# Two-head softmax denominators: one broadcast per head, and new hop lengths for the order planner

## The chip, the cores and the metric

The kernel runs on one core of a Trainium2 chip. The metric is the device time of one execution in microseconds (us), and lower is better. The engines of the core are PE (TensorE, matmuls), DVE (VectorE), ACT (ScalarE), POOL (GpSimd) and SP (SyncE), which issues every DMA of this kernel from one queue. Each engine takes its instructions in the order in which they stand in its own program, and an instruction that waits holds up all behind it on that engine.

## What is computed

Causal attention over 2 batches of 12 heads (448 tokens, head size 64), followed by two feed-forward networks on 896 tokens of width 768, all in float32:

```
scores = q @ k.T / 8, masked above the diagonal, minus the row maximum
attn   = exp(scores) / (sum(exp(scores)) + 1e-9)
x      = attn @ v                      # heads side by side: 896 x 768
xn     = x / sqrt(mean(x*x) + 1e-6) * rms_g
y      = (silu(xn @ w_gate) * (xn @ w_val)) @ w_out     # inner width 1536
h      = y @ w_in
out    = max(0.01*h, h) @ w_out2                        # inner width 2048
```

The weights arrive as float64 and are turned on the chip into pairs of float32 (a high and a low part); each product of the two networks is three matmuls.

## The kernel before, in words

**Attention.** The 24 heads are worked on as 12 pairs; pairs 0 to 5 are batch 0, pairs 6 to 11 batch 1. One pair i passes through these steps:

1. `load_pair`: SP loads `qk` (448 KB) and `v` (256 KB) into one of five buffers. `round_pair`: ACT casts q and k (L268).
2. `maxima` (L281, L289): PE multiplies q by k into two PSUM banks, DVE takes masked row maxima into `m`. `maxima_rows`: PE transposes them (L315), DVE copies them to `mt` (L318), SP writes them to DRAM (`md`, L320) and reads them back as one row for each head (`mrow`, L324).
3. `exponents`: PE adds the row of maxima (L339) and the product k by q (L343), ACT takes the exponential into `p` (L364), POOL clears what lies beyond the diagonal (L370, L374).
4. `attend`: PE sums `p` over keys by a matmul with ones (L401) and multiplies `p` by v (L386). ACT copies the sums to `sm` (L421). Then comes a trip over DRAM which spreads the 2 x 448 sums over 64 partitions, so that the reciprocal is short, and spreads the results over all partitions: SP stores `sd` (L423) and loads `st` in two transfers (L427); DVE adds and takes the reciprocal into `r` (L431, L434); SP stores `rd` (L436) and loads the broadcast `rb` (L439): 128 partitions, 64 with the 448 values of each head. POOL multiplies the pair's output by `rb` (L446), ACT squares it (L454), and POOL adds the squares to `acc` (L457). The last pair has its reciprocals taken on DVE (L416, L418), without this trip.

Such a trip is four transfers, each of which waits for the one before: sums to `sd`, `sd` to `st`, `r` to `rd`, `rd` to `rb`. Buffers of this trip are rings of four: `rd_134` and `rb_138` belong to pairs 0, 4 and 8, `rd_135` and `rb_139` to 1, 5 and 9, `rd_136` and `rb_140` to 2, 6 and 10, `rd_137` and `rb_141` to 3 and 7.

**Norm.** After the last pair of a batch, `norm` sums `acc` over partitions on PE (L475), goes over DVE, POOL, PE (L482) and ACT to a scale for each token, and DVE, ACT and POOL write `xn` (L502 to L512).

**Networks.** Matmuls at L571, L572 and L573, eighteen for a block of 128 outputs of one batch. The first four weight blocks (`hl_69` to `hl_72`) are loaded and converted during attention. Their 72 matmuls for batch 0 need only the norm of batch 0, so PE has them to do while batch 1 ends. Those for batch 1 begin after the second norm, and the further weights are converted by ACT, DVE and POOL (L187 to L197) from then on.

**What sets the order.** No engine program is written out by hand. Every step is handed to a planner (`Order`) with its engine, a cost, a rank, and `late`, the time from the end of an issue until its result is there. `emit` plays the program with these numbers, always takes the step that can start first (of those ready, the one of lowest rank), and emits the instructions in that order. At run time the engines keep the order, and wait for each other by semaphores only. So a changed cost or `late` moves instructions on all engines.

Of the kernel before, what the change touches and what calls it, by code (L numbers as in the profile page):

```python
# [18 lines left out]
class Order:  # L19
# [12 lines left out]
    def add(self, eng, cost, fn, r=(), w=(), rank=0.0, late=0.0, mode=None, at=0.0):  # L32
        n = len(self.steps)
        deps = set()
        for k in r:
            deps.update(self.written.get(k, ()))
        for k in w:
            deps.update(self.written.get(k, ()))
            deps.update(self.read.get(k, ()))
        for k in w:  # L40
            self.written[k] = [n]
            self.read[k] = []
        for k in r:
            if k not in w:
                self.read.setdefault(k, []).append(n)
        self.steps.append((eng, cost, fn, deps, rank, late, mode, at))
        return n
# [48 lines left out]
def causal_attention_two_ffns(  # L96
# [23 lines left out]
    nc = tc.nc  # L120
    P = 128
    NPAIR, _, _, S = qk.shape
    D = 64
# [14 lines left out]
    add = od.add  # L138
# [15 lines left out]
    late = {}  # L154
# [17 lines left out]
    def weight(key, rank, at=0.0):  # L172
        n = slot[key]
        src = queue[n][1]
        w = src.shape[1]
        raw, x, hl = raws[n % NRAW], xs32[n % NX], hls[n % NHL]
        kr, kx, kh = ("raw", n % NRAW), ("x", n % NX), ("hl", n % NHL)
        words = raw.bitcast(U32).rearrange("p (n t) -> p n t", t=2)
        top, low = words[:, :w, 1], words[:, :w, 0]
        tf = raw.bitcast(F32).rearrange("p (n t) -> p n t", t=2)[:, :w, 1]  # L180
        xb = x.bitcast(U32)[:, :w]
        add("SP", 0.5, lambda: nc.sync.dma_start(out=raw[:, :w], in_=src),
            w=[kr], rank=rank - 30, late=6.0, at=at)

        add("ACT", 0.85, lambda: nc.scalar.activation(x[:, :w], tf, AF.Abs), r=[kr], w=[kx], rank=rank)  # L187
        add("DVE", 0.62, lambda: nc.vector.tensor_scalar(  # L188
            x[:, :w], x[:, :w], LEAST, MOST, ALU.max, ALU.min), r=[kx], w=[kx], rank=rank)
        add("DVE", 0.6, lambda: nc.vector.tensor_scalar(  # L190
            xb, xb, 3, 0x3FFFFFF8, ALU.logical_shift_left, ALU.bitwise_and), r=[kx], w=[kx], rank=rank)
        add("DVE", 1.0, lambda: nc.vector.scalar_tensor_tensor(  # L192
            xb, top, 0xC0000000, xb, ALU.bitwise_and, ALU.bitwise_or), r=[kr, kx], w=[kx], rank=rank)
        add("DVE", 1.0, lambda: nc.vector.scalar_tensor_tensor(  # L194
            xb, low, 29, xb, ALU.logical_shift_right, ALU.bitwise_or), r=[kr, kx], w=[kx], rank=rank)
        add("ACT", 0.85, lambda: nc.scalar.copy(hl[:, 0, :w], x[:, :w]), r=[kx], w=[kh], rank=rank)  # L196
        add("POOL", 1.95, lambda: nc.gpsimd.tensor_tensor(  # L197
            out=hl[:, 1, :w], in0=x[:, :w], in1=f32(hl[:, 0, :w]), op=ALU.subtract),
            r=[kx, kh], w=[kh], rank=rank)
# [13 lines left out]
    NQ, NR, NM, NB = 5, 3, 4, 4  # L213
# [5 lines left out]
    mt = ring(NM, [2 * NC, C], F32R, "mt")  # L219
    md = ring(NM, [2, NC, C], F32, "md", dram)  # L220
# [5 lines left out]
    sms = ring(2, [P, S], F32, "sm")  # L226
# [3 lines left out]
    sd = ring(NB, [2, 2, QA, QB], F32, "sd", dram)  # L230
    sts = ring(NB, [2 * QA, 2, QB], F32, "st")
    rs = ring(NB, [2 * QA, QB], F32, "r")
    rd = ring(NB, [2, QA, QB], F32, "rd", dram)
    rbs = ring(NB, [P, S], F32, "rb")
# [9 lines left out]
    SP, ST, AV, SM = banks[0:2], banks[2:6], banks[6], banks[7]  # L244
# [14 lines left out]

    def load_pair(i, at):  # L260
        add("SP", 0.5, lambda: nc.sync.dma_start(out=qks[i % NQ], in_=qk[i]),
            w=[("qk", i % NQ)], rank=10 * i - 30, late=3.0, at=at)
        add("SP", 0.5, lambda: nc.sync.dma_start(out=vs[i % NQ], in_=v[i]),
            w=[("v", i % NQ)], rank=10 * i - 20, late=3.0, at=at)

    def round_pair(i):
        t, o = qks[i % NQ], qkr[i % NR]
# [44 lines left out]
    def maxima_rows(i):  # L312
        keys = [("m", i % NM, j, c) for j in range(2) for c in range(NC)]
        m = m32[i % NM]
        add("PE", 0.12, lambda: nc.tensor.transpose(  # L315
            out=SM[:2 * NC, :C], in_=m.rearrange("p j c -> p (j c)"), identity=ident[:C, :C]),
            r=keys, w=["sm"], rank=10 * i - 29, mode=128)
        add("DVE", 0.15, lambda: nc.vector.tensor_copy(mt[i % NM], SM[:2 * NC, :C]),  # L318
            r=["sm"], w=[("mt", i % NM)], rank=10 * i - 29)
        add("SP", 0.45, lambda: nc.sync.dma_start(  # L320
            out=md[i % NM].rearrange("j c p -> (j c) p"), in_=f32(mt[i % NM])),
            r=[("mt", i % NM)], w=[("md", i % NM)], rank=10 * i - 160, late=2.1)
        for j in range(2):
            add("SP", 0.4, lambda j=j: nc.sync.dma_start(  # L324
                out=f32(MS[i % NM][j * D:j * D + 1, :]),
                in_=md[i % NM][j].rearrange("c p -> (c p)").unsqueeze(0)),
                r=[("md", i % NM)], w=[("ms", i % NM, j)], rank=10 * i - 160, late=2.1)

    def exponents(i):
        t = qks[i % NQ]  # L330
# [47 lines left out]
    def attend(i):  # L378
        b, hp = divmod(i, NP)
        x = x32[:, hp, b * S:(b + 1) * S]  # L380
# [28 lines left out]
        for kb in range(KB):  # L409
            add("PE", pw[kb] * 0.00165 + 0.04, lambda kb=kb: values(kb),  # L410
                r=[("p", i % 2, 0, kb), ("p", i % 2, 1, kb), ("v", i % NQ)], w=["av"], rank=10 * i + 5,
                mode=128)
        if last:
            for h in range(2):
                n = slice(h * S // 2, (h + 1) * S // 2)
                add("DVE", 0.4, lambda n=n: nc.vector.tensor_scalar(  # L416
                    rbs[i % NB][:, n], SM[:, n], 1e-9, None, ALU.add), r=["sm"], w=[("rb", i % NB, h)], rank=0)
                add("DVE", 1.9, lambda n=n: nc.vector.reciprocal(rbs[i % NB][:, n], rbs[i % NB][:, n]),  # L418
                    w=[("rb", i % NB, h)], rank=0)
        else:  # L420
            add("ACT", 0.57, lambda: nc.scalar.copy(sms[i % 2], SM[:, :S]), r=["sm"], w=[("sms", i % 2)],  # L421
                rank=10 * i + 5)
            add("SP", 0.45, lambda: nc.sync.dma_start(  # L423
                out=sd[i % NB].rearrange("j h a b -> (j h) (a b)"), in_=sms[i % 2][0:P:32, :]),
                r=[("sms", i % 2)], w=[("sd", i % NB)], rank=10 * i - 60, late=2.1)
            for j in range(2):
                add("SP", 0.45, lambda j=j: nc.sync.dma_start(  # L427
                    out=sts[i % NB][j * QA:(j + 1) * QA], in_=sd[i % NB][j].rearrange("h a b -> a h b")),
                    r=[("sd", i % NB)], w=[("sts", i % NB, j)], rank=10 * i - 60, late=2.1)
            st = sts[i % NB]  # L430
            add("DVE", 0.15, lambda: nc.vector.scalar_tensor_tensor(  # L431
                out=rs[i % NB], in0=st[:, 0], scalar=1e-9, in1=st[:, 1], op0=ALU.add, op1=ALU.add),
                r=[("sts", i % NB, 0), ("sts", i % NB, 1)], w=[("r", i % NB)], rank=10 * i - 20)
            add("DVE", 0.25, lambda: nc.vector.reciprocal(rs[i % NB], rs[i % NB]),  # L434
                w=[("r", i % NB)], rank=10 * i - 20)
            add("SP", 0.45, lambda: nc.sync.dma_start(  # L436
                out=rd[i % NB].rearrange("j a b -> (j a) b"), in_=rs[i % NB]),
                r=[("r", i % NB)], w=[("rd", i % NB)], rank=10 * i - 60, late=2.1)
            add("SP", 0.45, lambda: nc.sync.dma_start(  # L439
                out=rbs[i % NB],  # L440
                in_=rd[i % NB].rearrange("j a b -> j (a b)").unsqueeze(1).to_broadcast([2, D, S])),
                r=[("rd", i % NB)], w=[("rb", i % NB)], rank=10 * i - 60, late=2.4)
        if i + 1 < NPAIR:
            add("ACT", 0.57, lambda: nc.scalar.copy(x, AV[:, :S]), r=["av"], w=[("x", b, hp)],
                rank=10 * i + 5)
            add("POOL", 1.1, lambda: nc.gpsimd.tensor_tensor(out=x, in0=x, in1=rbs[i % NB], op=ALU.mult),  # L446
                r=[("rb", i % NB)], w=[("x", b, hp)], rank=10 * i + 26)
        else:
            add("DVE", 0.65, lambda: nc.vector.tensor_tensor(
                out=x, in0=AV[:, :S], in1=rbs[i % NB], op=ALU.mult),  # L450
                r=["av", ("rb", i % NB, 0), ("rb", i % NB, 1)], w=[("x", b, hp)], rank=10 * i + 26)
        a = acc[:, b * S:(b + 1) * S]
        sq = sqs[i % 2] if hp else a
        add("ACT", 0.57, lambda: nc.scalar.activation(sq, x, AF.Square), r=[("x", b, hp)],  # L454
            w=[("sq", i % 2) if hp else ("acc", b)], rank=10 * i + 27)
        if hp:
            add("POOL", 1.1, lambda: nc.gpsimd.tensor_tensor(out=a, in0=a, in1=sq, op=ALU.add),  # L457
                r=[("sq", i % 2)], w=[("acc", b)], rank=10 * i + 27)
# [315 lines left out]
```

## Time and profile before

| what | value |
|---|---|
| median of 3 runs | 679.12 us (675.7 to 685.01) |
| the profiled execution | 676.31 us |
| its span, first to last instruction | 674.6 us |
| time outside the span | 1.7 us |
| PE busy | 630.5 us, 93% of the span |
| DVE, ACT, POOL busy | 395.7, 249.8, 198.8 us |
| mean granted PE clock | 0.947 of full speed |
| DMA | 68.26 MB, mean 101 GB/s |

The profile's time line falls into three stages: attention up to about 167 us, the second norm and the start of the networks up to about 209 us, and from there to the end a stretch of matmuls. A granted clock of 1.00 is 2.4 GHz, 0.50 is 1.2 GHz. A row of the time line gives the start, the duration, engine, line, operation, tiles and count, and in brackets how long the engine stood idle before it and what ended that.

### The profile page before, as it was taken

How to read it: one execution, taken by the hardware profiler on the slowest of the kernel's cores; microseconds unless marked ns; L12 is line 12 of the kernel's file. 1: busy time of each engine (PE TensorE's matmuls, PEld its weight loads, DVE VectorE, ACT ScalarE, POOL GpSimd, SP SyncE). 2: the span in 40 equal slices, each digit the busy share in tenths (PEclk: the TensorE clock that was granted, in tenths of full speed). 3: DMA queues.
4: the chain of work that ended last, by engine and by line, in shares of the span. 5: the costliest groups of instructions: out<-in, count | busy, mean ns of one | idle time of the engine just before them, and what ended most of it. 6: DMA issues, size and time to landing. Idle time of an engine off the chain costs nothing.

```text
span 674.6 us, 8621 instructions
## 1 busy us (share of the span) xinstructions
PE 630.5 (93%) x3280; PEld 542.0 (80%) x3280; DVE 395.7 (59%) x668; ACT 249.8 (37%) x410; POOL 198.8 (29%) x158
## 2 busy tenths in 40 slices
PE   7968968799399999999999999999999999999997
PEld 4544445467388999999999999999999999999997
DVE  6665424513279977655666445579999984443400
ACT  3553423431154343333432332345455452232210
POOL 0154324542323232223232222233233222323210
PEclk9896777789689999999999999999999999999999
DMA  7362221002304432333224232223223324334000
GB/s 249 116 184 67 82 71 32 30 17 62 108 12 175 142 141 101 133 116 119 94 93 141 97 134 97 95 94 137 98 93 123 97 78 138 111 133 153 28 27 29
DMA packets 19848, 68.26 MB, mean 101 GB/s; under 512 B 4762, under 2 KB 7774, under 8 KB 19806
## 3 DMA queue, kind: packets, MB, share of 16 engines
q1 hardware_dynamic: 19806, 67.70, 30.2%
q8 instruction: 26, 0.43, 0.3%
q14 instruction: 16, 0.13, 0.1%
HBM read 64.78 MB, written 2.91 MB: 100 GB/s over the span
## 4 chain that ended last, share of the span: by engine, by line
PE 68%; DVE 2%; issue 0%; ACT 0%; POOL 0%; POOLq 0%; ACTq 0%
PE bank L573 23%; PE bank L571 23%; PE bank L572 23%; DVE x L192 1%; POOL hl L197 0%; DVE x L194 0%; DVE T L630 0%; DVE sg L625 0%; ACT T L628 0%; ACT sg L623 0%; DVE x L190 0%; DVE x L188 0%; ACT sg L724 0%; POOLq L197 0%; ACTq L724 0%
## 5 line engine op out<-in xcount | busy, mean ns | idle before, releaser
L197 POOL TENSOR_TENSOR hl<-x,hl 128x768 fp32r<-128x768 f32 (+1 forms) x70 | 139.4, 1992 | 340.0 <-ACT hl L196 334.6
L571 PE MATMUL bank<-xn,hl 128*128 128x448 f32 x288 | 107.3, 372 | 1.9 <-ACT xn L505 1.9
L572 PE MATMUL bank<-xn,hl 128*128 128x448 f32 x288 | 107.0, 372 | 1.5 <-POOL xn L512 1.1
L573 PE MATMUL bank<-xn,hl 128*128 128x448 f32 x288 | 106.6, 370 | 0.3 <-POOL hl L197 0.3
L187 ACT ACTIVATE x<-raw 128x768 f32<-128x768 f32 (+1 forms) x70 | 61.8, 884 | 104.8 <-POOL hl L197 104.8
L188 DVE TENSOR_SCALAR x<-x 128x768 f32<-128x768 f32 (+1 forms) x70 | 39.4, 562 | 93.8 <-ACT x L187 93.8
L192 DVE SCALAR_TENSOR_TENSOR x<-raw,x 128x768 uint32<-128x768 uint32 (+1 forms) x70 | 87.0, 1243 | 2.2
L196 ACT CAST hl<-x 128x768 fp32r<-128x768 f32 (+1 forms) x70 | 56.8, 812 | 48.5 <-PE bank L572 44.8
L573 PE MATMUL bank<-y,hl 128*128 128x448 f32 x192 | 70.1, 365 | 0.0
L571 PE MATMUL bank<-y,hl 128*128 128x448 f32 x192 | 70.1, 365 | 0.0
L572 PE MATMUL bank<-G,hl 128*128 128x448 f32 x192 | 70.1, 365 | 0.0
L571 PE MATMUL bank<-G,hl 128*128 128x448 f32 x192 | 70.1, 365 | 0.0
L573 PE MATMUL bank<-G,hl 128*128 128x448 f32 x192 | 70.1, 365 | 0.0
L572 PE MATMUL bank<-y,hl 128*128 128x448 f32 x192 | 70.1, 365 | 0.0
L194 DVE SCALAR_TENSOR_TENSOR x<-raw,x 128x768 uint32<-128x768 uint32 (+1 forms) x70 | 65.4, 934 | 1.1
L572 PEld LDWEIGHTS bank<-xn,hl 128*128 128x128 f32 x288 | 55.2, 192 | 6.8 <-POOL xn L512 1.4
L571 PEld LDWEIGHTS bank<-xn,hl 128*128 128x128 f32 x288 | 55.1, 191 | 6.6 <-ACT xn L505 2.1
L573 PEld LDWEIGHTS bank<-xn,hl 128*128 128x128 f32 x288 | 55.1, 191 | 5.0 <-POOL hl L197 0.6
L289 DVE CUSTOM_DVE_ANT_0 bank<-bank,maskw 112x224 f32<-112x224 f32 (+2 forms) x96 | 42.2, 466 | 28.5 <-PE bank L281 27.2
L572 PE MATMUL bank<-T,hl 128*128 128x448 f32 x144 | 52.6, 365 | 0.0
L571 PE MATMUL bank<-T,hl 128*128 128x448 f32 x144 | 52.6, 365 | 0.0
L573 PE MATMUL bank<-T,hl 128*128 128x448 f32 x144 | 52.6, 365 | 0.0
(79 smaller groups left out, 939.3 us busy)
## 6 DMA issues: line engine op xcount, KB each, us to landing
raw<-in_out SPq DMA_DIRECT2D x24, 768.0 KB
raw<-in_in SPq DMA_DIRECT2D x16, 768.0 KB
raw<-in_gate SPq DMA_DIRECT2D x12, 768.0 KB
raw<-in_val SPq DMA_DIRECT2D x12, 768.0 KB
qk<-in_qk SPq DMA_DIRECT2D x12, 448.0 KB
v<-in_v SPq DMA_DIRECT2D x12, 256.0 KB
raw<-in_out SPq DMA_DIRECT2D x6, 512.0 KB
out<-sg SPq DMA_DIRECT2D x12, 224.0 KB
```

Of the source, the lines that this page charges most:

```text
L187: add("ACT", 0.85, lambda: nc.scalar.activation(x[:, :w], tf, AF.Abs), r=[kr], w=[kx], rank=rank)
L188: add("DVE", 0.62, lambda: nc.vector.tensor_scalar(x[:, :w], x[:, :w], LEAST, MOST, ALU.max, ALU.min), r=[kx], w=[kx], rank=rank)
L192: add("DVE", 1.0, lambda: nc.vector.scalar_tensor_tensor(xb, top, 0xC0000000, xb, ALU.bitwise_and, ALU.bitwise_or), r=[kr, kx], w=[kx], ra ...
L194: add("DVE", 1.0, lambda: nc.vector.scalar_tensor_tensor(xb, low, 29, xb, ALU.logical_shift_right, ALU.bitwise_or), r=[kr, kx], w=[kx], ra ...
L196: add("ACT", 0.85, lambda: nc.scalar.copy(hl[:, 0, :w], x[:, :w]), r=[kx], w=[kh], rank=rank)
L197: add("POOL", 1.95, lambda: nc.gpsimd.tensor_tensor(out=hl[:, 1, :w], in0=x[:, :w], in1=f32(hl[:, 0, :w]), op=ALU.subtract), r=[kx, kh], w ...
L289: nc.vector.tensor_tensor_reduce(out=s, in0=s, in1=maskw[:, S - w:S], scale=-1.0, scalar=3.0e38, op0=ALU.add, op1=ALU.min, accum_out=m[:, ...
L571: nc.tensor.matmul(o, hi, xh, start=s, stop=False, skip_group_check=True)
L572: nc.tensor.matmul(o, hi, xl, start=False, stop=False, skip_group_check=True)
L573: nc.tensor.matmul(o, lo, xh, start=False, stop=e, skip_group_check=True)
```

## The change

Two things. The broadcast `rb` is issued as two transfers, one for each head, each 64 partitions x 448 values read from the 448 values of that head in DRAM; before, one transfer had 2 x 64 x 448 as its shape, head first. The multiplication on POOL waits for both. And the `late` values handed to the planner are others: 1.3 instead of 2.1 for the short transfers, 1.6 instead of 2.4 for `rb`, 4.2 instead of 6.0 for weights, 3.2 instead of 3.0 for `qk` and `v`. The instructions besides are the same, and one SP issue a pair is added for eleven pairs.

```diff
             add("SP", 0.45, lambda: nc.sync.dma_start(
                 out=rd[i % NB].rearrange("j a b -> (j a) b"), in_=rs[i % NB]),
-                r=[("r", i % NB)], w=[("rd", i % NB)], rank=10 * i - 60, late=2.1)
-            add("SP", 0.45, lambda: nc.sync.dma_start(
-                out=rbs[i % NB],
-                in_=rd[i % NB].rearrange("j a b -> j (a b)").unsqueeze(1).to_broadcast([2, D, S])),
-                r=[("rd", i % NB)], w=[("rb", i % NB)], rank=10 * i - 60, late=2.4)
+                r=[("r", i % NB)], w=[("rd", i % NB)], rank=10 * i - 60, late=1.3)
+
+            for j in range(2):
+                add("SP", 0.45, lambda j=j: nc.sync.dma_start(
+                    out=rbs[i % NB][j * D:(j + 1) * D],
+                    in_=rd[i % NB][j].rearrange("a b -> (a b)").unsqueeze(0).to_broadcast([D, S])),
+                    r=[("rd", i % NB)], w=[("rb", i % NB, j)], rank=10 * i - 60, late=1.6)
...
             add("POOL", 1.1, lambda: nc.gpsimd.tensor_tensor(out=x, in0=x, in1=rbs[i % NB], op=ALU.mult),
-                r=[("rb", i % NB)], w=[("x", b, hp)], rank=10 * i + 26)
+                r=[("rb", i % NB, 0), ("rb", i % NB, 1)], w=[("x", b, hp)], rank=10 * i + 26)
...
         add("SP", 0.5, lambda: nc.sync.dma_start(out=raw[:, :w], in_=src),
-            w=[kr], rank=rank - 30, late=6.0, at=at)
+            w=[kr], rank=rank - 30, late=4.2, at=at)
```

The order moves on every engine in the attention stage. Three places matter to the prediction. The first is SP near the end of attention, from the sums of pair 8 (`rd_134`) to the `rb` of pair 9 (`rb_139`), as a difference (- before, + the change; `sd`, `st`, `rd`, `rb` are the four transfers of a trip):

```order
+L436 DMA rd_134<-r_130 64x14
 L320 DMA md_115<-mt_111 8x112
-L436 DMA rd_134<-r_130 64x14
+L441 DMA rb_138<-rd_134 64x448 x2
+L324 DMA mrow_103<-md_115 1x448 x2
 L423 DMA sd_123<-sm_121 4x448
-L324 DMA mrow_103<-md_115 1x448 x2
-L439 DMA rb_138<-rd_134 128x1x448
 L427 DMA st_127<-sd_123 32x2x14 x2
+L423 DMA sd_124<-sm_120 4x448
 L436 DMA rd_135<-r_131 64x14
```

Before, the broadcast of pair 8 goes out directly ahead of the `st` of pair 9, and the `sd` of pair 10 behind `rd_135`; in the change the two broadcasts stand ahead of the last `mrow` and of `sd_123`, and `sd_124` stands ahead of the wait for `r_131`.

The second is DVE at pair 6 (`r_132`), between the last row maximum of pair 9 (`m_105`) and the first of pair 10 (`m_106`):

```order
 L289 ISA bank_74,m_105<-bank_74,maskw 112x112
 L289 ISA m_105 112x1
-L318 CAST mt_109<-bank_80 8x112
-L489 TENSOR_SCALAR ms_157<-bank_75 112x4
 L431 SCALAR_TENSOR_TENSOR r_132<-st_128 64x14
 L434 RECIPROCAL r_132<-r_132 64x14
+L318 CAST mt_109<-bank_80 8x112
+L491 TENSOR_SCALAR ms_157<-bank_75 112x4
 L289 ISA bank_73,m_106<-bank_73,maskw 112x448
```

The sum that waits for `st` now stands ahead of the copy `mt`, from which the row of maxima sets out; before it stood behind it.

The third is SP at pair 3 (`rd_137`), where the row of maxima of pair 6 (`mrow_102`) is fetched:

```order
+L436 DMA rd_137<-r_133 64x14
 L320 DMA md_114<-mt_110 8x112
-L436 DMA rd_137<-r_133 64x14
+L441 DMA rb_141<-rd_137 64x448
 L324 DMA mrow_102<-md_114 1x448 x2
+L441 DMA rb_141<-rd_137 64x448
 L423 DMA sd_122<-sm_120 4x448
 L261 DMA qk_87<-in_qk 128x896
-L439 DMA rb_141<-rd_137 128x1x448
 L427 DMA st_126<-sd_122 32x2x14 x2
```

One half of the broadcast, with its wait for `rd`, is now ahead of `mrow_102`, and the `sd` of the next pair follows the other half. On PE, 57 of the 72 network matmuls for batch 0 stand ahead of the second norm's L475 in the change and 63 before; 30 and 27 of them stand ahead of the sums of the last pair.

## Rows read from the trace of the kernel before

**Rows 1.** The page: the PE clock granted in 40 slices of the span

```profile
PEclk9896777789689999999999999999999999999999
```

**Rows 2.** Stretches: start:end, length, busy us (count) by engine, clock, DMA share, GB/s

```profile
45.50:167.20 121.70, 99.80 (x638) 63.96 (x636) 49.82 (x162) 42.73 (x91) 46.57 (x63) 0.79 0.18 54
48.30:54.60 6.30, 3.62 (x22) 1.72 (x24) 5.24 (x14) 2.16 (x4) 3.17 (x5) 0.50 0.34 98
126.70:140.20 13.50, 12.20 (x58) 7.37 (x58) 7.45 (x28) 6.46 (x14) 7.74 (x10) 0.50 0.06 19
29.30:45.50 16.20, 15.78 (x144) 9.98 (x142) 12.89 (x39) 13.20 (x27) 8.76 (x10) 1.00 0.52 144
75.90:88.10 12.20, 11.43 (x103) 7.34 (x102) 5.37 (x20) 5.05 (x12) 2.52 (x5) 1.00 0.27 80
209.00:671.00 462.00, 461.85 (x2278) 427.95 (x2278) 292.49 (x370) 167.30 (x253) 128.10 (x65) 1.00 0.32 107
```

**Rows 3.** Time line of PE: start, us, line, tiles, count [idle before <- what ended it]

```profile
59.13 0.91 PE L339 MATMUL bank<-mrow,onesr 64*128 64x448 f32 x2 [2.60 <-DMA mrow<-md]
65.77 1.93 PE L401 MATMUL bank<-p,ones 128*32 128x448 f32 x16
77.15 1.07 PE L401 MATMUL bank<-p,ones 128*32 128x448 f32 x16
84.29 1.07 PE L401 MATMUL bank<-p,ones 128*32 128x448 f32 x16
127.23 0.35 PE L315 MATMUL bank<-ident,m 112*8 112x112 f32 x1 [3.53 <-DVE m L289]
156.11 1.95 PE L401 MATMUL bank<-p,ones 128*64 128x448 f32 x16
176.51 1.65 PE L475 MATMUL bank<-ones,acc 128*112 128x2 f32 x8 [9.22 <-POOL acc L457]
184.40 0.53 PE L571 MATMUL bank<-xn,hl 128*128 128x448 f32 x1 [1.94 <-ACT xn L505]
209.15 0.47 PE L573 MATMUL bank<-xn,hl 128*128 128x448 f32 x1 [0.26 <-POOL hl L197]
```

**Rows 4.** DVE's waits for `st`: us, times, longest; and the last pair's product

```profile
DVE r L431 <- DMA st<-sd: 40.5, 7, 11.1
165.95 0.62 DVE L449 TENSOR_TENSOR x<-bank,rb 128x448 f32<-128x448 f32 x1
```

**Rows 5.** Time line of SP's queue: start of the issue, us that the issue took

```profile
59.48 0.79 SPq L427 DMA_DIRECT2D st<-sd  x2
61.98 0.47 SPq L436 DMA_DIRECT2D rd<-r  x1
133.26 0.52 SPq L423 DMA_DIRECT2D sd<-sm  x1
135.44 0.79 SPq L427 DMA_DIRECT2D st<-sd  x2
153.85 0.54 SPq L439 DMA_DIRECT2D rb<-rd  x1
154.49 0.88 SPq L427 DMA_DIRECT2D st<-sd  x2
162.15 0.48 SPq L436 DMA_DIRECT2D rd<-r  x1
163.86 0.53 SPq L439 DMA_DIRECT2D rb<-rd  x1
```

**Rows 6.** The page's DMA issues, and stretches with a broadcast alone and a `v` load

```profile
rb<-rd SPq DMA_DIRECT2D x11, 224.0 KB
147.00:149.50 2.50, 2.50 (x28) 1.40 (x26) 0.00 (x0) 1.44 (x4) 0.00 (x0) 1.00 0.14 50
77.50:78.00 0.50, 0.50 (x16) 0.36 (x8) 0.50 (x3) 0.50 (x2) 0.50 (x1) 1.00 0.67 258
```

**Rows 7.** Time line of POOL: the last multiplication by a broadcast

```profile
172.31 1.13 POOL L446 TENSOR_TENSOR x<-x,rb 128x448 f32<-128x448 f32 x1 [8.64 <-DMA rb<-rd]
```

More of the change, by code (lines that the diff above doesn't have):

```diff
@@ L261, in load_pair @@
         add("SP", 0.5, lambda: nc.sync.dma_start(out=qks[i % NQ], in_=qk[i]),
-            w=[("qk", i % NQ)], rank=10 * i - 30, late=3.0, at=at)
+            w=[("qk", i % NQ)], rank=10 * i - 30, late=3.2, at=at)
         add("SP", 0.5, lambda: nc.sync.dma_start(out=vs[i % NQ], in_=v[i]),
-            w=[("v", i % NQ)], rank=10 * i - 20, late=3.0, at=at)
+            w=[("v", i % NQ)], rank=10 * i - 20, late=3.2, at=at)
     def round_pair(i):
@@ L321, in maxima_rows @@
             out=md[i % NM].rearrange("j c p -> (j c) p"), in_=f32(mt[i % NM])),
-            r=[("mt", i % NM)], w=[("md", i % NM)], rank=10 * i - 160, late=2.1)
+            r=[("mt", i % NM)], w=[("md", i % NM)], rank=10 * i - 160, late=1.3)
         for j in range(2):
@@ L326, in maxima_rows @@
                 in_=md[i % NM][j].rearrange("c p -> (c p)").unsqueeze(0)),
-                r=[("md", i % NM)], w=[("ms", i % NM, j)], rank=10 * i - 160, late=2.1)
+                r=[("md", i % NM)], w=[("ms", i % NM, j)], rank=10 * i - 160, late=1.3)
     def exponents(i):
@@ L424, in attend @@
                 out=sd[i % NB].rearrange("j h a b -> (j h) (a b)"), in_=sms[i % 2][0:P:32, :]),
-                r=[("sms", i % 2)], w=[("sd", i % NB)], rank=10 * i - 60, late=2.1)
+                r=[("sms", i % 2)], w=[("sd", i % NB)], rank=10 * i - 60, late=1.3)
             for j in range(2):
@@ L428, in attend @@
                     out=sts[i % NB][j * QA:(j + 1) * QA], in_=sd[i % NB][j].rearrange("h a b -> a h b")),
-                    r=[("sd", i % NB)], w=[("sts", i % NB, j)], rank=10 * i - 60, late=2.1)
+                    r=[("sd", i % NB)], w=[("sts", i % NB, j)], rank=10 * i - 60, late=1.3)
             st = sts[i % NB]
```

## The prediction, made before the changed kernel was run

> **What bounds the kernel now.** I read the page's slices first. The granted clock is full from the middle of the span on, and broken before that [rows 1]. The stretches say why the second part cannot gain: from 209 to 671 us PE is busy 461.85 of 462.00 us at clock 1.00 [rows 2]. Nothing that the change touches runs there, so a gain has to come from starting that stretch earlier.
>
> Before it lies attention. From 45.5 to 167.2 us PE is busy 99.8 of 121.7 us at a mean clock of 0.79 [rows 2]: 21.9 us idle. Five stretches between 48.3 and 140.2 us run at 0.50, the lower level of 1.2 GHz; together they are 50.0 us long with 43.6 us of matmuls (the first and the last stand in [rows 2]). They set in around idle times of PE, as those of 2.60 us that ended at 59.13 and of 3.53 us that ended at 127.23 [rows 3]. The same sixteen sum matmuls take 1.93 us at the low level and 1.07 at the high one [rows 3], so 0.446 of 43.6 us, 19.4 us, are the price of the low clock.
>
> What lies behind the idle times? DVE waited 40.5 us for `st` in seven waits, up to 11.1 us long [rows 4], and its row maxima, on which PE waits, stand behind these waits; PE waits for `mrow` as well [rows 3]. Both are transfers of a few KB. SP's queue shows what holds them. With no broadcast ahead, `st` at 59.48 is followed by `rd` at 61.98 us: 2.50 us for `st`, the sum and the reciprocal. With a broadcast issued 0.64 us ahead, at 153.85, the same way from `st` at 154.49 to `rd` at 162.15 takes 7.66 us [rows 5]. While a broadcast runs alone, 50 GB/s move at a DMA share of 0.14, a good two of the sixteen engines; a `v` load, also of rows of some 2 KB, moves 258 GB/s [rows 6]. So 224 KB [rows 6] take 4.6 us, and small transfers which have a piece on these two engines wait behind it.
>
> **The change, step by step.**
>
> *The broadcast in two.* Its outer dimension was 2, and two engines' worth of traffic is what the row shows. Now each half has 64 rows outermost. At the rate of the `v` load 224 KB take 0.9 us instead of 4.6. The trace of before has no one-row source read by more engines, so the price has two ends: 0.9 us, or 9.2 us if each half lands on a single engine at 25 GB/s. I take 0.9, since the `v` load is nearest in size and rows, and its destination too begins with partitions. In sentences apart: the Trainium skill's page "DMA: Bandwidth & Descriptors", section "Rules for kernel authors", speaks against the change: transfers to disjoint halves of the partitions are not worth it, both spread over all sixteen engines, and one transfer is better. By that rule alone the first term below would be zero. Its premise does not hold here, since the share of 0.14 [rows 6] shows a transfer that is not spread. The same page, section "Why a DMA increments its semaphore by 16 and not by 1", says that the slowest dimension sets how many engines serve a transfer; with 2 the trace agrees, with 64 no run here shows it yet.
>
> *One more issue.* An issue of a broadcast takes 0.54 us [rows 5], eleven times 5.9 us on SP. SP mostly waits in this stage, so I put it into the loop below and not on the path by itself.
>
> *First term, attention.* If no `st` or `mrow` is held, the 21.9 us of idle time and the 19.4 us of low clock go: 41.3 us. What is late next? SP's queue takes the trips one after the other: `sd` to `st` 2.18 us (133.26 to 135.44), `st` to `rd` 2.50, `rd` to `rb` 1.71 (162.15 to 163.86), two issues 1.08 [rows 5]: 7.5 us a pair. From one pair's sums to the next at full clock PE needs 7.14 us (77.15 to 84.29) [rows 3]. The two are close, and in the new order some rows stand behind more than before: at pair 3 `mrow_102` comes behind one half of a broadcast and its wait for `rd`, and at pair 6 the copy `mt` comes behind the sum that waits for `st`. Each such place costs between nothing and about 1.7 us, the wait from `rd` to `rb`. I take back 1.0 us for each of the nine pairs from 45 us on, 9 us. The undisturbed stretches bound it from below: 0.42 us idle in 16.2 and 0.77 in 12.2 us [rows 2], some 3 us for nine pairs. From above 3 us a pair, if loads which wait for PE stand in the loop. One low-clock stretch may stay: of the two shown the one holds 3.62, the other 12.20 us of matmuls [rows 2], which cost 1.6 and 5.4 us at 0.446; I take 3 us. First term: 41.3 - 9 - 3 = 29.3 us.
>
> *Second term, the end of attention.* The sums of the last pair begin at 156.11 and the second norm's first matmul only at 176.51, after 9.22 us without work [rows 3]. Two broadcasts hold it. The reciprocals of the last pair stand on DVE behind the sum that waits for the `st` of pair 10, whose `rd` went out only at 162.15; and the last `rb`, issued at 163.86 [rows 5], reached POOL at 172.31 [rows 7]. Without them DVE takes the reciprocals as soon as the sums are there: 1.95 us of sums [rows 3], 4.4 us on DVE (from 162.15 to the end of the last product at 165.95 + 0.62 [rows 4]), and 3.1 us for a square and the sums into `acc` (from the end of POOL's product at 172.31 + 1.13 [rows 7] to 176.51), so 9.5 us. Of PE's work for batch 0, 27 network matmuls fill that time. The norm up to the first matmul of batch 1 stays a chain of 7.9 us (176.51 to 184.40), and so does the conversion behind it, whose last part PE awaits from POOL at 209.15 [rows 3]: ACT, DVE and POOL set it, whatever PE's clock is. So all of it starts 20.4 - 9.5 = 10.9 us sooner at best. I take 10, because a late `rb` of pair 10 can stand in for some of it; bounds 8 and 11.
>
> *Everything else.* The weights' `late` of 4.2 orders issues in the last stretch, where PE is busy 100%; nothing.
>
> **Sum.** 29.3 + 10 = 39.3 us from the profiled execution's 676.3 us gives 637. The median of the three runs, 679.1, lies 2.8 us above that execution; I add 1 and say 638 us.
>
> **The rivals.**
>
> *A: SP's queue becomes the bound.* Nine pairs at 3 us more than PE needs: 27 to 30 us come back of the 41.3, and the end gains 8. Then 676 - 12 - 8 = 656 us. For it: 7.5 against 7.14 us leaves no slack, and loads that wait for PE stand in the same queue. Against it: the trips overlap over three pairs, and PE kept 97% and 94% busy in the two stretches at full clock [rows 2].
>
> *B: the split does not speed the broadcast up.* Both halves then use the engines that the whole one used: the 224 KB move at the same 50 GB/s, the second half starts 0.54 us later, and the waits stay: 676 to 682 us, the latter with all eleven issues on the path. Against it speaks that two engines' worth is not all that rows of this size get [rows 6]. The Trainium skill's rule on halves ("DMA: Bandwidth & Descriptors", "Rules for kernel authors") comes to this case.
>
> *C, slower: each half on one engine.* The source is a single row, read 64 times; if that confines a half to one engine, 224 KB take 9.2 us one behind the other, 4.6 more than now, and whatever is queued behind it is later by so much. Seven waits for `st` [rows 4] and the end: 8 x 4.6 = 37 us, 713 us. It decides once the two halves together take longer than today's 4.6 us. Nothing in the trace excludes it, but the nearest load does not behave so.
>
> **How the numbers follow.** Forecast 0.78, A 0.12, B 0.06, C 0.04. The forecast's own range runs from 41.3 - 3 + 11 = 49 us gained, 627, to 41.3 - 25 + 8 = 24 gained, 652; half of A brings the upper end to 656. So 626 to 656 holds a good 0.8. A change of 2% is 13.6 us, about what a measurement of this kernel can tell, as its three runs spread by 9 us. Forecast and A lie below 665.5: faster 0.90. B is no change: 0.06. C is slower: 0.04.
>
> **What would show it.** In the profile after, a broadcast alone should run at a share well above 0.14 for about a microsecond, DVE's waits for `st` should fall from 40.5 to under 20 us, the slices of the clock should show 9 nearly throughout attention, sums of neighbouring pairs should lie 8 to 9 us apart, and the second norm's L475 counterpart should follow the last sums by 9 to 11 us. The stretch to the end should still be 462 us long. I am wrong if PE stays idle for other waits (`mrow`, SP's queue behind a load), if the clock stays low without long gaps, or if the share of 0.14 stays.

## The result, and the profile after

The changed kernel takes 647.81 us (median of 4 runs, 645.13 to 651.63) against 677.84 us for the kernel before: a ratio of 0.954, with an interval from 0.945 to 0.963. In a second set it took 644.1 against 675.98 us, 0.952 with an interval from 0.950 to 0.954. The forecast was 638 us, in a range from 626 to 656. Ratios and their intervals leave out runs that took over 1.5% longer than the fastest of the same kernel; medians do not. The profiled execution took 649.4 us with a span of 647.7; beside the 676.31 us of before that is 26.9 us less, where 39.3 were forecast.

The first view is the page's line of granted clock in 40 slices, the answer to [rows 1]:

```profile
PEclk9887876998999999999999999999999999999999
```

The second norm starts 26 us earlier (176.51 to 150.38), but the clock is not full in attention. The next view is the table by stretches, with the columns of [rows 2]:

```profile
45.50:143.00 97.50, 86.59 (x611) 53.76 (x613) 45.02 (x163) 44.05 (x93) 45.14 (x64) 0.86 0.24 70
62.00:68.00 6.00, 5.67 (x27) 2.13 (x29) 3.01 (x11) 1.36 (x2) 2.82 (x2) 0.50 0.46 122
102.70:112.70 10.00, 9.98 (x56) 7.91 (x58) 3.35 (x14) 1.90 (x5) 2.61 (x4) 0.50 0.11 27
128.20:129.60 1.40, 1.40 (x17) 0.81 (x13) 0.00 (x0) 0.23 (x1) 1.10 (x4) 1.00 0.44 166
182.00:644.00 462.00, 462.00 (x2281) 428.00 (x2279) 291.95 (x370) 166.98 (x254) 127.70 (x64) 1.00 0.32 107
```

The last row is the stretch that could not gain: PE is busy for all of its 462 us, as before. The fourth is a broadcast, both halves, with no other transfer beside it but two rows of 1.8 KB: 166 GB/s at a share of 0.44, against 50 GB/s at 0.14 in [rows 6]. Another, from 136.4 to 138.0 us, moves at 142 GB/s. The first has 10.9 us of idle time (97.50 - 86.59) where the stage of before had 21.9, and a clock of 0.86 where it had 0.79. (The stage of before, up to 167.2 us, takes in 11.1 us of work at full clock behind the start of its last sums.)

PE's time line, to be held against [rows 3], shows the idle times that are left and the end of attention:

```profile
49.95 0.26 PE L315 MATMUL bank<-ident,m 112*8 112x112 f32 x1 [2.54 <-DVE m L289]
...
62.33 0.35 PE L315 MATMUL bank<-ident,m 112*8 112x112 f32 x1 [2.46 <-DVE m L289]
...
72.87 1.07 PE L401 MATMUL bank<-p,ones 128*32 128x448 f32 x16 [1.01 <-DVE mt L318]
...
86.29 0.89 PE L339 MATMUL bank<-mrow,onesr 64*128 64x448 f32 x2 [1.82 <-DMA mrow<-md]
...
141.20 1.95 PE L401 MATMUL bank<-p,ones 128*64 128x448 f32 x16
...
150.38 0.85 PE L477 MATMUL bank<-ones,acc 128*112 128x2 f32 x8
...
157.19 0.74 PE L573 MATMUL bank<-xn,hl 128*128 128x448 f32 x1 [1.94 <-ACT xn L507]
...
181.09 0.47 PE L575 MATMUL bank<-xn,hl 128*128 128x448 f32 x1 [0.79 <-POOL hl L197]
```

No idle time in attention reaches 3 us. The second norm's first matmul (L477, which was L475) follows the last sums by 9.18 us and without a wait; before it was 20.40 us, 9.22 of them idle. The gain, place by place: the last sums begin 14.9 us earlier (156.11 to 141.20), the way from there to the first matmul of batch 1 is 12.3 us shorter (28.29 to 15.99), and the next row of the list, the wait for the first converted weight, adds 0.85. That makes 28.1 us at 181.09; 1.2 us are lost again behind it.

DVE's waits for `st`, the answer to [rows 4], have fallen from 40.5 to 18.3 us:

```profile
DVE r L431 <- DMA st<-sd: 18.3, 7, 6.5
```

And SP's queue near the end of attention, with POOL's product, the answers to [rows 5] and [rows 7]:

```profile
134.09 0.97 SPq L427 DMA_DIRECT2D st<-sd  x2
...
136.92 0.47 SPq L436 DMA_DIRECT2D rd<-r  x1
...
138.76 1.08 SPq L441 DMA_DIRECT2D rb<-rd  x2
...
142.87 1.14 POOL L448 TENSOR_TENSOR x<-x,rb 128x448 f32<-128x448 f32 x1 [2.27 <-DMA rb<-rd]
```

From `st` to `rd` it takes 2.83 us, with a broadcast's issue (1.13 us at 135.20) in between; before it was 7.66 us. Part of this is the order, since before the broadcast was issued ahead of that `st` and here behind it; the split alone is read from e1 below. From the first half of the broadcast to POOL's product it takes 4.11 us, before 8.45.

### The profile page after: what moved, and what is told of

Same layout as the page of the kernel before. It is cut to its first block, busy times and chain, and to the rows that moved or that the text cites. A ratio compares the mean times of both kernels' runs of the same rounds, so it can differ in the third digit from the quotient of the medians.

```text
span 647.7 us, 8644 instructions
## 1 busy us (share of the span) xinstructions
PE 623.2 (96%) x3280; PEld 537.4 (83%) x3280; DVE 393.6 (61%) x668; ACT 250.1 (39%) x410; POOL 196.1 (30%) x158
## 4 chain that ended last, share of the span: by engine, by line
PE 90%; DVE 3%; issue 3%; DMA 3%; POOL 1%; ACT 1%; SPq 0%; POOLq 0%; DVEq 0%; ACTq 0%
PE bank L573 25%; PE bank L575 25%; PE bank L574 25%; PE bank L386 4%; PE bank L343 3%; PE bank L401 2%; PE bank L281 2%; PE bank L339 2%; DVE bank L289 1%; DMA st<-sd 1%; PE bank L524 1%; POOL hl L197 1%; DVE x L504 1%; PE bank L484 0%; DMA rb<-rd 0%
## 5 line engine op out<-in xcount | busy, mean ns | idle before, releaser
L192 DVE SCALAR_TENSOR_TENSOR x<-raw,x 128x768 uint32<-128x768 uint32 (+1 forms) x70 | 85.0, 1215 | 2.3
L194 DVE SCALAR_TENSOR_TENSOR x<-raw,x 128x768 uint32<-128x768 uint32 (+1 forms) x70 | 65.1, 929 | 1.1
```

The source lines that it names most:

```text
L192: add("DVE", 1.0, lambda: nc.vector.scalar_tensor_tensor(xb, top, 0xC0000000, xb, ALU.bitwise_and, ALU.bitwise_or), r=[kr, kx], w=[kx], ra ...
L194: add("DVE", 1.0, lambda: nc.vector.scalar_tensor_tensor(xb, low, 29, xb, ALU.logical_shift_right, ALU.bitwise_or), r=[kr, kx], w=[kx], ra ...
```

## The experiments

Two theories stood against each other at first. **E:** a transfer whose first dimension is 2 is served by two DMA engines (an estimate from the share of 0.14 of sixteen; no view shows which), so the broadcast was slow and held the small transfers behind it; the split gives each half 64 rows outermost. **O:** the new hop lengths, and the order that comes of them, brought the gain. Beside them stood **N:** two transfers run faster than one whatever their shape.

The table has all kernels. Each ratio is to the kernel before in the same set, whose medians were 675.65 to 677.84 us. "Idle" is PE's idle time from 29 us to the start of the last sums, and "low clock" is 0.446 of PE's busy time at clock 0.50 there, the price used in the prediction; both are summed over windows of 1 us in each kernel's own trace, a window of mixed clock by its share. e9 is the same kernel as e12, whose trace stands for both.

| kernel | median us | ratio to before | idle | low clock | last sums at |
|---|---|---|---|---|---|
| before | 677.84 | 1 | 22.3 | 19.9 | 156.11 |
| changed, first set | 647.81 | 0.954 (0.945 to 0.963) | 11.7 | 12.8 | 141.20 |
| changed, second set | 644.10 | 0.952 (0.950 to 0.954) | 10.6 | 9.0 | 136.05 |
| e1, split alone | 640.55 | 0.948 (0.945 to 0.950) | 8.7 | 10.2 | 133.63 |
| e2, hop lengths alone | 687.50 | 1.016 (1.013 to 1.019) | 37.6 | 22.0 | 176.72 |
| e3, two by columns | 684.22 | 1.012 (1.009 to 1.014) | 28.5 | 16.9 | 162.18 |
| e4, one row as source | 641.25 | 0.948 (0.946 to 0.950) | 10.2 | 5.9 | 133.66 |
| e5, split, big hops new | 642.59 | 0.948 (0.941 to 0.955) | 6.6 | 7.6 | 131.01 |
| e6, split, short hops new | 648.25 | 0.960 (0.957 to 0.962) | 13.8 | 10.4 | 141.83 |
| e7, split, `st` told 3.6 us | 638.26 | 0.944 (0.942 to 0.947) | 7.1 | 7.5 | 129.31 |
| e8, e7 with a half from ACT | 643.65 | 0.954 (0.951 to 0.957) | 6.9 | 10.0 | 132.93 |
| e9, e7 with big hops new | 637.72 | 0.942 (0.935 to 0.949) | - | - | - |
| e10, e7 with weights later | 646.33 | 0.957 (0.954 to 0.959) | 9.9 | 9.9 | 135.76 |
| e12, e9 with more runs | 634.15 | 0.938 (0.935 to 0.941) | 6.3 | 3.0 | 125.79 |

What is left of each stretch once idle time and low clock are taken off lies between 84.9 and 88.7 us in every row. So nearly all by which the kernels differ in attention is in these two.

**e1 and e2: each part of the change alone.** e1 is the changed kernel with the old values, of which two stand here (likewise 3.0 for `qk` and `v`, and 2.1 for the other short transfers):

```diff
-            w=[kr], rank=rank - 30, late=4.2, at=at)
+            w=[kr], rank=rank - 30, late=6.0, at=at)
...
-                    r=[("rd", i % NB)], w=[("rb", i % NB, j)], rank=10 * i - 60, late=1.6)
+                    r=[("rd", i % NB)], w=[("rb", i % NB, j)], rank=10 * i - 60, late=2.4)
```

> The broadcast as two transfers, with the hop lengths (late) of the kernel before. Theory E (a transfer whose first dimension is 2 is served by two DMA engines, one whose first dimension is 64 by all; the small transfers behind it stop waiting; the hop lengths only shift places in the queues): most of the 28 us come, 646 to 658 us, and the broadcast from issue to POOL takes 3.4 to 4.3 us as in the changed kernel, not 7.4 to 8.5. Rival O (the order that the new hop lengths give is the cause): 672 to 680 us. If both matter, 658 to 668.

e2 is the kernel before with the new values:

```diff
-            w=[kr], rank=rank - 30, late=6.0, at=at)
+            w=[kr], rank=rank - 30, late=4.2, at=at)
...
-                r=[("rd", i % NB)], w=[("rb", i % NB)], rank=10 * i - 60, late=2.4)
+                r=[("rd", i % NB)], w=[("rb", i % NB)], rank=10 * i - 60, late=1.6)
```

> The new hop lengths with the single broadcast of the kernel before. Theory E: the broadcast still takes 7.4 us or more from issue to POOL, DVE still waits around 40 us for st, 670 to 682 us; the planner now believes in shorter trips than there are, so slower than before is as likely as faster. Rival O: 646 to 656 us.

The split alone gained 35.1 us, more than the change, and the hop lengths alone lost 11.9 us. O falls. E had the sign but not the size: it expected 646 to 658 us of e1, which took 640.55, and 670 to 682 us of e2, which took 687.50, since it put less on the hop lengths than they cost. At the third broadcast from the end, e1's SP queue has the order of [rows 5], a broadcast directly ahead of `st`:

```profile
121.52 1.11 SPq L441 DMA_DIRECT2D rb<-rd  x2
122.71 1.00 SPq L427 DMA_DIRECT2D st<-sd  x2
...
126.71 0.48 SPq L436 DMA_DIRECT2D rd<-r  x1
```

From `st` to `rd` it takes 4.00 us there, with an `sd` and half an `st` of the next pair in between, against 7.66 before. What the new lengths do with a slow broadcast shows in e2's waits of PE (us, times, longest):

```profile
PE bank L339 <- DMA mrow<-md: 30.1, 9, 6.4
```

A planner that is told of shorter trips puts the small transfers close together, and at run time the row `mrow`, for which PE waits, lands late behind a broadcast. Of e2's SP queue and of its PE, one such place:

```profile
98.36 0.55 SPq L439 DMA_DIRECT2D rb<-rd  x1
98.96 0.77 SPq L324 DMA_DIRECT2D mrow<-md  x2
...
105.83 0.91 PE L339 MATMUL bank<-mrow,onesr 64*128 64x448 f32 x2 [5.84 <-DMA mrow<-md]
```

The broadcast goes out 0.60 us ahead of the row of maxima, which PE has 6.87 us after its issue. Before, DVE had borne the waits, 40.5 us for `st`; in e2 it waits 32.1 us, and PE, which sets the time, has taken on the rest.

**e3 and e4: the shape or the number of transfers.** e3 keeps the change's order and its two transfers but cuts by columns, so that each has 2 x 64 x 224 as its shape:

```diff
-                    out=rbs[i % NB][j * D:(j + 1) * D],
-                    in_=rd[i % NB][j].rearrange("a b -> (a b)").unsqueeze(0).to_broadcast([D, S])),
+                    out=rbs[i % NB][:, j * (S // 2):(j + 1) * (S // 2)],
+                    in_=rd[i % NB].rearrange("k a b -> k (a b)")[:, j * (S // 2):(j + 1) * (S // 2)]
+                    .unsqueeze(1).to_broadcast([2, D, S // 2])),
```

> The changed kernel's order and number of transfers, but the two transfers take 224 columns of both heads each instead of 448 columns of one head, so that the first dimension of each is 2 again. Theory E: both stay on two engines, DMA share near 0.14 while they run alone, 4.3 us or more for the two, DVE's waits for st back near 40 us, 668 to 684 us. Rival N (two transfers at once run faster than one, whatever their shape): 646 to 652 us, as the changed kernel.

e4 is one transfer with 128 rows outermost, all from the first head's row; the second head's factors are left out.

```diff
-            for j in range(2):
...
-                    out=rbs[i % NB][j * D:(j + 1) * D],
-                    in_=rd[i % NB][j].rearrange("a b -> (a b)").unsqueeze(0).to_broadcast([D, S])),
+                out=rbs[i % NB],
+                in_=rd[i % NB][0].rearrange("a b -> (a b)").unsqueeze(0).to_broadcast([P, S])),
```

> One transfer of the same 224 KB with a first dimension of 128: all 128 partitions take the row of the first head (the second head's 1/sum is left out). Theory E: it is spread over all engines, 3.4 to 4.3 us from issue to POOL, and the time is that of the changed kernel or up to 6 us less, since eleven issues of 0.54 us go: 642 to 650 us. Rival N: the single transfer stays slow, 668 to 680 us.

e3 lost the whole gain with two transfers, and e4 kept it with one: the shape decides, and N falls. (By their numbers, e3 lies at the upper edge of what E expected and e4 0.75 us under it.) The stretches of a broadcast alone say the same; first e3, then e4:

```profile
150.00:153.00 3.00, 2.77 (x32) 1.50 (x24) 0.00 (x0) 0.00 (x0) 0.00 (x0) 1.00 0.13 41
```

```profile
127.80:129.30 1.50, 1.50 (x13) 1.05 (x11) 0.40 (x2) 0.24 (x1) 0.00 (x0) 1.00 0.42 146
```

The share is 0.13 with a first dimension of 2, and 0.42 with 128. How the slow shape holds others shows in e3's SP queue, at the end of attention:

```profile
159.07 1.12 SPq L441 DMA_DIRECT2D rb<-rd  x2
160.78 0.50 SPq L436 DMA_DIRECT2D rd<-r  x1
...
166.85 1.04 SPq L441 DMA_DIRECT2D rb<-rd  x2
```

The last `rb` waits for `rd`, a transfer of 3.5 KB. Its issue ended at 161.28, and 5.57 us passed until the next issue, with the earlier broadcast on its way. In the changed kernel the same hop takes 1.37 us (from 136.92 + 0.47 to 138.76).

The Trainium skill's page "DMA: Bandwidth & Descriptors" says in "Rules for kernel authors" that transfers to disjoint halves of the partitions are not worth it. Here two such halves gained 35 us over a whole that moved at a share of 0.14; the measurement decides. The advice in the same table of the Trainium skill to put the partitions outermost agrees with e4 (a share of 0.42), as its section "Why a DMA increments its semaphore by 16 and not by 1", which the prediction cited, does with the shares of e3 and e4.

**e5, e6 and the change again: which hop lengths cost.** e1 was faster than the change. Two theories: **S**, that the short hops of 1.3 and 1.6 us put `r` and what is behind it too early; **W**, that the weights' and loads' new lengths do. e5 takes the short hops of the changed kernel back, e6 the big ones:

```diff
-                r=[("rd", i % NB)], w=[("rb", i % NB, j)], rank=10 * i - 60, late=1.6)
+                r=[("rd", i % NB)], w=[("rb", i % NB, j)], rank=10 * i - 60, late=2.4)
```

```diff
-            w=[kr], rank=rank - 30, late=4.2, at=at)
+            w=[kr], rank=rank - 30, late=6.0, at=at)
```

> The split, with the new hop lengths of the big loads alone (weights 4.2, qk and v 3.2) and the old 2.1 and 2.4 of the small transfers. The split alone took 640.6 us, the change as a whole 647.8. Theory S (the short hops of 1.3 and 1.6 us make the planner put the sum r and the rows behind it on DVE and SP too early, before st is there): the time is that of the split alone, 638 to 643 us. Rival W (the big loads' new lengths put the second weight's load behind v and ahead of the row md that PE needs, which costs the 5.5 us by which the change is behind the split alone at the third sums): 645 to 650 us.

> The split, with the new hop lengths of the small transfers alone (1.3 and 1.6) and the old 6.0 and 3.0 of the big loads. Its SP queue has the second weight's load behind v as the whole change has. Theory S: 645 to 650 us, as the whole change. Rival W: 638 to 643 us.

> The changed kernel once more, beside the others on one chip: 645 to 651 us. If it lies at 640 here, the difference to the split alone was one of chips or runs and not of the order.

e6, with the short hops alone, is as slow as the change or slower (648.25 us). e5, with the big ones alone, has an interval that spans the split alone. S holds. W falls by e6, not by e5, two of whose four runs (645.96 and 647.37 us) lie where W expected them. Ratio against ratio, the new short hops cost 1.2% beside the split alone, some 8 us; with the big ones as well it is 0.5 to 0.7%, 3 to 5 us; beside the short hops the big ones are thus a gain. The place can be read on DVE in the changed kernel, where the sum `r` stands among the row maxima:

```profile
45.11 0.13 DVE L289 DVE_READ_ACCUMULATOR2_ANT m<- 112x1 f32 x1
48.51 0.17 DVE L431 SCALAR_TENSOR_TENSOR r<-st 64x14 f32<-64x14 f32 x1 [3.27 <-DMA st<-sd]
...
48.87 0.25 DVE L289 CUSTOM_DVE_ANT_0 bank<-bank,maskw 112x112 f32<-112x112 f32 x1
```

Three of the pair's maxima stand behind a wait of 3.27 us for `st`, and PE's transposition of them is the matmul at 49.95 with 2.54 us of idle time. That `st` was issued at 43.23 us, and the load of a weight right behind it at 44.08. In e1 the sum of the same pair stands behind the last of these maxima, and waits 0.33 us:

```profile
42.58 0.14 DVE L289 DVE_READ_ACCUMULATOR2_ANT m<- 112x1 f32 x1
...
43.47 0.69 DVE L431 SCALAR_TENSOR_TENSOR r<-st 64x14 f32<-64x14 f32 x1 [0.33 <-DMA st<-sd]
```

**e7: the sum later.** e1, with one value changed:

```diff
-                    r=[("sd", i % NB)], w=[("sts", i % NB, j)], rank=10 * i - 60, late=2.1)
+                    r=[("sd", i % NB)], w=[("sts", i % NB, j)], rank=10 * i - 60, late=3.6)
```

> The split alone (old hop lengths), but the planner is told 3.6 us instead of 2.1 for st. On DVE the row maxima and the copy mt then stand ahead of the sum r that waits for st at most pairs. Theory S, taken further: DVE's waits for st (16.9 us in the split alone) fall below 8 us, PE's waits for m and mt (3.6 us) fall, and the low clock behind them with it: 632 to 638 us. Rival: rb and with it x come later, POOL and acc hold the norms, or PE waits for mrow instead: 640 to 646 us.

638.26 us lies just above what S expected, and its interval overlaps with that of e1. DVE's waits for `st` fell only to 15.4 us, not below 8: they are fewer (4 instead of 5) but not shorter. PE's waits for `m` and `mt` came to 4.2 us; in e1 they were 5.1 by its list of waits, not 3.6 as the expectation has it. So the gain, if it is one, came only in part in the way that was expected.

**e8: one half from ACT's queue.** In e7:

```diff
-                add("SP", 0.45, lambda j=j: nc.sync.dma_start(
+                add("ACT" if j else "SP", 0.45, lambda j=j: (nc.scalar if j else nc.sync).dma_start(
                     out=rbs[i % NB][j * D:(j + 1) * D],
```

> As e7_sum_later (638.3 us), with the second head's broadcast issued from ACT's queue instead of SP's: eleven issues of 0.54 us leave SP and stand among ACT's exponentials, and ACT waits there for rd. Theory Q (SP's queue is still part of what holds st, md and mrow, as the transfer of one issue suggests, which was some 3 us faster than the change as a whole): 633 to 637 us. Rival: ACT's wait for rd holds the exponentials and PE behind them: 640 to 650 us.

It is 5.4 us slower than e7, so the rival has it, but hardly by ACT's wait for `rd`: ACT's list of waits has one of 2.1 us, and PE's idle time did not grow. The last sums come 3.6 us later, with 10.0 instead of 7.5 us of low clock, and the way from there to L477 takes 15.4 us. The order is a different one there: on DVE the sum `r` of pair 10 now stands behind the last pair's reciprocals. Of e8, DVE, ACT, POOL and PE:

```profile
138.69 0.10 DVE L431 SCALAR_TENSOR_TENSOR r<-st 64x14 f32<-64x14 f32 x1
...
140.74 0.47 ACTq L441 DMA_DIRECT2D rb<-rd  x1
...
144.12 1.16 POOL L448 TENSOR_TENSOR x<-x,rb 128x448 f32<-128x448 f32 x1 [7.71 <-DMA rb<-rd]
...
148.34 0.85 PE L477 MATMUL bank<-ones,acc 128*112 128x2 f32 x7 [2.63 <-POOL acc L459]
```

What the issues on SP cost is therefore not settled. e4, with eleven fewer than the change, is 0.4% below its second set, 2 to 3 us, and the two intervals just overlap.

**e10: the weights later.**

```diff
-        weight(key, 40.0 + 10 * n, at=20.0 + 8 * n)
+        weight(key, 40.0 + 10 * n, at=60.0 + 8 * n)
```

> As e7_sum_later, with the first four weights' loads and conversions allowed 40 us later (the planner's times 60 to 84 us instead of 20 to 44). Theory B (a load of 768 KB ahead of st, and conversions of the weights ahead of the row maxima on DVE, made the long waits for st between 40 and 62 us and PE's idle times there): no DVE wait for st over 4 us before 65 us, PE idle under 1 us between 40 and 65 us (e7: 3 us), 634 to 638 us. Rival: the same waits come later, where the conversions now stand, and network matmuls that fill PE's gaps are missing: 638 to 646 us.

The rival has it. The fifth sums came at 60.26 us instead of e7's 65.14, so the weights do hold the first pairs. But the conversions then lay at 65 to 101 us and held the later ones; one of the new idle times of PE:

```profile
76.35 0.26 PE L315 MATMUL bank<-ident,m 112*8 112x112 f32 x1 [1.96 <-DVE m L289]
```

At the last sums e10 was 6.5 us behind e7.

**e9 and e12: the fastest order.** e7 with 4.2 and 3.2 us for the big loads, in four and then in six runs:

```diff
-            w=[kr], rank=rank - 30, late=6.0, at=at)
+            w=[kr], rank=rank - 30, late=4.2, at=at)
```

> As e7_sum_later, with the new 4.2 and 3.2 us of the big loads. If those are worth nothing, as the split with them alone was (642.6 against 640.6 us, with intervals that overlap): 636 to 642 us; the time should follow the idle time of PE up to the last sums and its time at clock 0.50 there, 7.1 us and 7.5 us in e7_sum_later.

> The fastest order so far (the split, 3.6 us for st, 4.2 and 3.2 us for the big loads) once more, with more runs, since its first four spread from 633.3 to 644.5 us. 633 to 638 us, against 640.6 for the split alone and 644 to 648 for the change as a whole; PE idle up to the last sums 5 to 8 us and the low clock's price there 5 to 8 us, against 11.7 and 12.8 us in the change.

634.15 us, a ratio of 0.938 with an interval below those of the split alone, of the change and of e7. Beside e7 the big loads' lengths thus gain 0.6%, some 4 us, as they do in the change beside e6 (0.952 and 0.960); in e5 beside e1 nothing of it shows. The low clock, 3.0 us, is less than the 5 to 8 that were expected. Of e12, the stretch up to the last sums, with the columns of [rows 2]:

```profile
29.00:127.00 98.00, 91.69 (x712) 57.97 (x706) 58.57 (x195) 54.66 (x114) 54.65 (x73) 0.97 0.30 88
```

and what is left of PE's wait for the maxima between 29 and 150 us, first in e12, then in the changed kernel between 29 and 170 us:

```profile
PE bank L315 <- DVE m L289: 0.2, 1, 0.2
```

```profile
PE bank L315 <- DVE m L289: 5.0, 2, 2.5
```

The clock is 0.97 there, against 0.86 in the changed kernel from 29 to 141 us. Since only the order differs between the two, the order is worth 10 us or more.

## Why the prediction was right, and where it was off

*The bound and the cause* were right. The stretch of 462 us stayed as long, and the shape behind the share of 0.14 was the cause: e3 brought the old time back by the shape alone, e4 took it away with one transfer. Rivals B and C fall with the share of 0.44.

*The price of a broadcast* was put at 0.9 us by the rate of the `v` load. It takes 1.4 to 1.6 us, at 166 and 142 GB/s, not much over half that rate; even so, 4.3 us of the way to POOL went, near the 3.7 us that the prediction's prices give.

*The first term* is where the forecast missed: 29.3 us against 14.9. The two causes of loss were named rightly, 42.2 us up to the last sums by the table, but 12 us were taken back (9 of idle time, 3 of low clock), and 24.5 stayed: 11.7 of idle time and 12.8 of low clock. So 2.7 us of the shortfall of 14.4 are idle time and 9.8 the clock; the remaining 2 us lie in the rest of the stretch, which grew by 2.8 us, less 0.9 us by which the table's loss is above the prediction's 41.3. The step that failed is "One low-clock stretch may stay". Five stayed from 29 us on, among them the ten microseconds from 102.7, behind an idle time of 1.5 us, and one from 34 to 38 us, behind no idle time longer than 0.66 us. The prediction's own last sentence had named it, a clock that stays low without long gaps, but the sum had one stretch at 3 us, between the prices of the two that it read.

*The second term* was 10 us with bounds of 8 and 11. It measured 11.2 us from the last sums to the norm, where 10.9 had been put as the best case, and 1.1 us more in the norm's chain, which had been taken as fixed. The chain came as described, and the last sum into `acc` ends at 150.09 us:

```profile
148.94 1.15 POOL L459 TENSOR_TENSOR acc<-acc,sq 128x448 f32<-128x448 f32 x1 [2.59 <-ACT sq L456]
```

PE had its 27 network matmuls to do until 150.38, so the chain and PE's own queue end within 0.3 us of each other, and a shorter chain alone would have gained no more. That this term came out above its bound took 2 us off the miss of the first.

*The order* was costed as a take-back of 1 us a pair, which held for the idle time (9 against 11.7 us). What the prediction did not do is set the two parts of the change against each other: its take-back lumps the queue's pace with the new order, and the weights' new length stands at nothing. The small transfers' new lengths are a loss, some 8 us beside the split; the big ones gave back some 4 to 5 us of it, and all together without the split lost 11.9. Had the order been e12's, 634 us, the forecast of 638 would have been 4 us too high.

*Rival A*, 656 us by a bound on SP's queue, did not happen as it was described. (In the range, nine pairs at 3 us stand as 25 us, where they are 27; the end of 656 does not hang on it.) Most neighbouring sums lie 7.8 to 14.6 us apart, but the long gaps stand at PE's waits above, not at a pace of the queue, and e12, with as many issues, takes 22 us less than A's 656.

*The checks named ahead*: the broadcast's share, DVE's waits under 20 us, L477 9 to 11 us behind the sums and the last stretch of 462 us came as forecast. A clock of 9 nearly throughout attention and sums 8 to 9 us apart did not.

Open stays why the same order and kernel takes 649.4 us in one profiled execution and 644.29 in another: their low clock differs by 3.8 of the 5.1 us. That idle time sets the low clock off is argued from the rows, not shown, and the table speaks against a simple link: e8 and e12 have 6.9 and 6.3 us of idle time, and 10.0 and 3.0 us of low clock.

## What to carry to other kernels

Look at the first dimension of a slow broadcast and at the DMA share while it runs alone; here a share of 0.14 held up not only the broadcast's own consumer but the small transfers behind it, a `rd` of 3.5 KB by some 4 us in e3. When a change has two parts, give each a term with its own sign: here the one gained 35 us, and the other gave some of it back. For this planner, the length of a hop that DVE waits for was better told long (2.1 or 3.6 us) than short (1.3): a sum placed too early held the row maxima behind it. How far 3.6 is better than 2.1 is less sure, since the intervals of e7 and e1 overlap.

## What the runs showed of the hardware that was not expected

The issue of one half of the broadcast, 64 partitions, takes SP about 0.55 us (two in 1.08 at 138.76), and that of e4's whole, 128 partitions from one row, 0.34 us:

```profile
126.85 0.34 SPq L440 DMA_DIRECT2D rb<-rd  x1
```

So more rows were not dearer to issue. And the clock can fall with PE busy. In e7, PE was busy 4.97 of 5.00 us at clock 1.00 and, a microsecond later, 5.00 of 5.00 at 0.50:

```profile
91.00:96.00 5.00, 4.97 (x53) 3.76 (x43) 2.46 (x10) 2.23 (x6) 2.64 (x4) 1.00 0.05 8
97.00:102.00 5.00, 5.00 (x19) 3.74 (x21) 3.74 (x12) 1.87 (x4) 2.10 (x2) 0.50 0.15 39
```

In the first of the two lie the small matmuls of the first norm, L477 at 93.66 us. No run here tells what set the fall off.
